# Token chunks of a channel attention with a gated feed-forward: twelve of 504 or 508 tokens instead of eleven of 512 and one of 448

## The chip, the cores and the metric

The kernel runs on one core of one Trainium2 chip. The metric is the device time of the execution in microseconds. A core has TensorE (PE: matmuls and their weight loads), VectorE (DVE), ScalarE (ACT), GpSimd (POOL) and SyncE (SP, which here issues the DMAs).

## The reference

Four batches of 6080 tokens and 256 channels. First an attention between channels, whose weights are a 256 x 256 matrix for each batch; then a feed-forward layer of width 2048 on every token.

```python
B, N, C = (4, 6080, 256)
qn = q / (np.linalg.norm(q, axis=1, keepdims=True) + 1e-06)
kn = k / (np.linalg.norm(k, axis=1, keepdims=True) + 1e-06)
s = kn.transpose(0, 2, 1) @ qn / tau
a = softmax(s)                      # [B, 256, 256]
x = (v @ a).reshape(B * N, C)
h = x @ w_in                        # w_in [256, 2048]
g = h * (1.0 / (1.0 + np.exp(-1.702 * h)))
return g @ w_out                    # w_out [2048, 256]
```

## The kernel before

**Layout.** Tokens run along the free dimension, channels and hidden units along the 128 partitions. `v` comes in transposed and the output leaves transposed. The attention matrix of a batch is folded into `w_in` (`weights`, line 413), so that the main loop computes hidden units straight from `v`. Every factor of a product is split into a high and a low part (`split`, lines 78 and 79: a cast on ScalarE and a subtraction on VectorE), and each product is three matmuls: high by high, high by low, low by high.

**Chunks.** The tokens of a batch are cut into chunks (line 62), 512 wide by `NCH`, with a last one of 448. `chunks[c]` is a pair of offset and width. All tiles for a chunk in SBUF and PSUM have room for 512 columns and are used up to the width `w`. `v_load` fetches a chunk of `v`, `v_split` splits it.

**The main loop.** `order` lists the slots of a batch: chunk by chunk, and for each the 16 blocks `f` of 128 hidden units. In the first batch the first two chunks go in turn, block by block. In each slot `hidden` issues six matmuls (line 456: two halves of the channels by three products), a sigmoid on ScalarE (line 462), a product on VectorE (line 463) and the split of the result into `gh` and `gl`. Two or three slots later `project` issues the six matmuls of line 484 (two halves of the output channels by three products), which add up over the 16 blocks in PSUM. After the last block the two halves are copied out (VectorE line 492, ScalarE line 494) and stored (line 496). A chunk is thus 16 slots of 12 matmuls.

**Side work.** `put` hangs other work on slots by their number: the load and split of the next chunk, the attention of the next batch (`prepare`, `score` with 512 and 256 columns at lines 285 and 294, norms, softmax, folded weights), and in the first batch the conversion of the 64-bit weights (lines 118 to 132). These numbers depend on `NCHUNK` and `NF` only.

**Order.** PE runs in the order that the code is written in (`manual_schedule` for PE). The other engines' order in the main loop is decided by the scheduler from its own estimate of the time line.

Of the kernel before, what the change touches and what calls it, by code (L numbers as in the profile page):

```python
# [22 lines left out]
NCH = 512  # L23
# [4 lines left out]
def channel_attention_then_glu(  # L28
# [21 lines left out]
    B, N, C = q.shape  # L50
# [8 lines left out]
    TAIL = N - T * P  # L59
    UT = 2  # L60
    RT = 4
    chunks = [(o, min(NCH, N - o)) for o in range(0, N, NCH)]
    NCHUNK = len(chunks)

    const = ctx.enter_context(tc.tile_pool(name="const", bufs=1))
    wp = ctx.enter_context(tc.tile_pool(name="wp", bufs=NG + 2))
# [546 lines left out]
    with tc.manual_schedule(engines={mybir.EngineType.PE}):  # L613
        for b in range(B):
            side = start if b == 0 else {}
            order = [(c, f) for c in range(NCHUNK) for f in range(NF)]
            if b == 0:
                order[: 2 * NF] = [(c, f) for f in range(NF) for c in range(2)]

            def put(s, fn, *a):  # L620
                side.setdefault(s, []).append((fn, a))

            for c in range(2 if b == 0 else 1, NCHUNK + (b + 1 < B)):
                at_v = (c - 1) * NF
                bc = (b, c) if c < NCHUNK else (b + 1, 0)
                if b == 0 and c == 2:
# [7 lines left out]
            if b + 1 < B:  # L634
# [26 lines left out]
                put(e + 16, nxt.transposes)  # L661
                total = NCHUNK * NF
                at_g = [total - 32, total - 24, total - NF + 5, total - NF + 10]
# [45 lines left out]
```

## Time and profile before

| | us |
|---|---|
| median of 3 runs | 2286.29 |
| lowest and highest | 2285.43, 2288.52 |
| the profiled execution | 2288.67 |
| its span, first to last instruction | 2286.9 |

A profile is one execution. Its page gives the busy time of each engine and the chain of work that ended last, followed back from the end. The views used below are the page, the groups of instructions by line with shapes kept apart (busy us, mean ns of one, idle time before), the waits of PE (us in total, times, longest), the busy time by stage (sum for PE, weight loads, VectorE, ScalarE, GpSimd, then PE's granted clock, the DMA share and GB/s), and the chain in order of time (start, length, what). Matmuls are pipelined: a matmul's own duration (391 ns at 512 columns) is longer than the distance from its start to the next one's start, so the pace is read from starts.

### The profile page before, as it was taken

The numbers are of one execution on the slowest core, as the hardware profiler recorded it, in microseconds if no ns is written. First come the engines' busy times: TensorE is split into PE (matmuls) and PEld (weight loads), VectorE is DVE, ScalarE is ACT, GpSimd is POOL, SyncE is SP. The second block draws the span as 40 slices with busy tenths as digits, with TensorE's granted clock in tenths as the row PEclk, the third lists the DMA queues.
The fourth block names the chain that finished last, engine by engine and source line by source line (L and its number), as shares of the span: only waits on it lengthen the run. The fifth ranks groups of instructions, "written<-read, shape, count | busy, mean of one in ns | idle before, by whom it ended". The sixth has DMA issues, their size and how long they took to land.

```text
span 2286.9 us, 27146 instructions
## 1 busy us (share of the span) xinstructions
PE 2277.1 (100%) x10256; PEld 1901.9 (83%) x10256; DVE 1379.7 (60%) x2073; ACT 1240.4 (54%) x2145; POOL 219.2 (10%) x160
## 2 busy tenths in 40 slices
PE   9999999999999999999999999999999999999999
PEld 7788888888888888888888888888888888888888
DVE  6976656755556665665555666666555555555554
ACT  6766555554555555555454555654554444444444
POOL 0012222200011222110000222300000000000000
PEclk9999999999999999999999999999999999999999
DMA  9311211100111112110011112110001000000000
GB/s 340 109 51 60 74 56 54 46 27 19 36 38 56 56 56 72 55 39 18 19 38 36 56 56 74 53 35 22 18 19 36 19 19 28 28 19 28 27 10 18
DMA packets 45812, 109.76 MB, mean 48 GB/s; under 512 B 4464, under 2 KB 7792, under 8 KB 45680
## 3 DMA queue, kind: packets, MB, share of 16 engines
q1 hardware_dynamic: 45680, 108.02, 14.1%
q8 instruction: 80, 1.31, 0.3%
q14 instruction: 52, 0.43, 0.1%
HBM read 83.10 MB, written 24.90 MB: 47 GB/s over the span
## 4 chain that ended last, share of the span: by engine, by line
PE 98%; DVE 1%; DMA 1%; ACT 0%; SPq 0%; issue 0%; ACTq 0%
PE ps_o L484 45%; PE ps_h L456 45%; PE s L285 3%; PE ps_w L413 2%; PE s L275 2%; PE s L294 1%; DMA raw_k<-in_k 0%; PE s_first L250 0%; DMA raw_q<-in_q 0%; DVE v_l L79 0%; SPq L206 0%; PE ps_n L312 0%; DVE gl L79 0%; DVE g L463 0%; ACT sq L238 0%
## 5 line engine op out<-in xcount | busy, mean ns | idle before, releaser
L79 DVE TENSOR_TENSOR gl<-g,gh 128x512 fp32r<-128x512 f32 (+1 forms) x768 | 548.2, 715 | 463.7 <-ACT gh L78 462.2
L78 ACT CAST gh<-g 128x512 fp32r<-128x512 f32 (+1 forms) x768 | 472.3, 615 | 503.5 <-DVE g L463 501.5
L463 DVE TENSOR_TENSOR g<-ps_h,g 128x512 f32<-128x512 f32 (+1 forms) x768 | 524.3, 684 | 345.6 <-ACT g L462 338.8
L462 ACT ACTIVATE g<-ps_h 128x512 f32<-128x512 f32 (+1 forms) x768 | 455.6, 593 | 419.7 <-PE ps_h L456 418.0
L456 PE MATMUL ps_h<-v_h,wh 128*128 128x512 f32 (+1 forms) x1536 | 596.9, 389 | 0.0
L484 PE MATMUL ps_o<-gl,wo_h 128*128 128x512 f32 (+1 forms) x1536 | 595.0, 387 | 1.4 <-DVE gl L79 1.4
L456 PE MATMUL ps_h<-v_l,wh 128*128 128x512 f32 (+1 forms) x1536 | 595.5, 388 | 0.0
L484 PE MATMUL ps_o<-gh,wo_h 128*128 128x512 f32 (+1 forms) x1536 | 594.8, 387 | 0.0
L456 PE MATMUL ps_h<-v_h,wl 128*128 128x512 f32 (+1 forms) x1536 | 594.9, 387 | 0.0
L484 PE MATMUL ps_o<-gh,wo_l 128*128 128x512 f32 (+1 forms) x1536 | 594.6, 387 | 0.0
L484 PEld LDWEIGHTS ps_o<-gl,wo_h 128*128 128x128 f32 x1536 | 288.3, 188 | 59.5 <-DVE gl L79 2.9
L456 PEld LDWEIGHTS ps_h<-v_h,wl 128*128 128x128 f32 x1536 | 288.3, 188 | 58.1 <-DVE wl L79 0.6
L484 PEld LDWEIGHTS ps_o<-gh,wo_h 128*128 128x128 f32 x1536 | 288.3, 188 | 57.9 <-ACT gh L78 0.5
L484 PEld LDWEIGHTS ps_o<-gh,wo_l 128*128 128x128 f32 x1536 | 288.3, 188 | 56.8
L456 PEld LDWEIGHTS ps_h<-v_h,wh 128*128 128x128 f32 x1536 | 288.6, 188 | 55.3
L456 PEld LDWEIGHTS ps_h<-v_l,wh 128*128 128x128 f32 x1536 | 288.7, 188 | 54.5
L240 POOL TENSOR_TENSOR acc_q<-acc_q,sq 128x512 f32<-128x512 f32 (+1 forms) x72 | 93.7, 1302 | 1110.8 <-ACT sq L238 1110.8
L240 POOL TENSOR_TENSOR acc_k<-acc_k,sq 128x512 f32<-128x512 f32 (+1 forms) x72 | 116.1, 1613 | 3.3 <-ACT sq L238 3.2
L79 DVE TENSOR_TENSOR v_l<-v_raw,v_h 128x512 fp32r<-128x512 f32 (+2 forms) x94 | 76.0, 847 | 4.6 <-ACT v_h L78 4.6
L285 PE MATMUL s<-qs,ks 128*128 128x512 f32 (+1 forms) x272 | 73.5, 390 | 0.0
L238 ACT ACTIVATE sq<-raw_q 128x512 f32<-128x512 f32 (+1 forms) x96 | 58.4, 609 | 21.4 <-DMA raw_q<-in_q 16.8
L238 ACT ACTIVATE sq<-raw_k 128x512 f32<-128x512 f32 (+1 forms) x96 | 58.1, 605 | 7.5 <-DMA raw_k<-in_k 3.3
(87 smaller groups left out, 896.3 us busy)
## 6 DMA issues: line engine op xcount, KB each, us to landing
v_raw<-in_vT SPq DMA_DIRECT2D x44, 512.0 KB, 3.8
out_T<-osb SPq DMA_DIRECT2D x88, 256.0 KB, 2.1
raw_q<-in_q SPq DMA_DIRECT2D x43, 512.0 KB, 3.8
raw_k<-in_k SPq DMA_DIRECT2D x43, 512.0 KB, 4.5
words<-in_w_in SPq DMA_DIRECT2D x8, 512.0 KB, 7.7
words<-in_w_out SPq DMA_DIRECT2D x8, 512.0 KB, 3.4
v_raw<-in_vT SPq DMA_DIRECT2D x4, 448.0 KB, 3.6
out_T<-osb SPq DMA_DIRECT2D x8, 224.0 KB, 2.0
```

What stands on the lines that cost most here:

```text
L78: ins = nc.scalar.copy(dst_hi, src)
L79: nc.vector.tensor_tensor(dst_lo, src, dst_hi.bitcast(F32), op=ALU.subtract)
L238: nc.scalar.activation(sq, r, AF.Square)
L240: eng.tensor_tensor(acc, acc, sq, op=ALU.add)
L275: nc.tensor.matmul(self.s[i][:, :C], lhsT=ks[:, j, i * P : (i + 1) * P], rhs=qs[:, j, :], start=u == start and j == 0, stop=last and j == ...
L285: nc.tensor.matmul(self.s[i], lhsT=ks[:pp, j, 0, i * P : (i + 1) * P], rhs=qs[:pp, j, :, :], start=u == start and j == 0, stop=False, skip ...
L294: nc.tensor.matmul(self.s[i][:, C:], lhsT=ks[:pp, j, 1, i * P : (i + 1) * P], rhs=qs[:pp, j, 0, :], start=False, stop=last and j == nt - 1 ...
L413: nc.tensor.matmul(ps, lhsT=l[:, j, ci], rhs=r[:, j, :], start=n == 0, stop=n == 3 * NC2 - 1,)
L456: nc.tensor.matmul(ps[:, :w], lhsT=l[:, j, fs], rhs=r[:, j, :w], start=n == 0, stop=n == 3 * NC2 - 1,)
L462: newest[0] = nc.scalar.activation(g, ps[:, :w], AF.Sigmoid, scale=1.702)
L463: nc.vector.tensor_tensor(g, ps[:, :w], g, op=ALU.mult)
L484: nc.tensor.matmul(out[d][:, :w], lhsT=l[:, f, ds], rhs=r[:, :w], start=f == 0 and n == 0, stop=f == NF - 1 and n == 2,)
```

## The change

The number of chunks is rounded up from the token count by 512, as before twelve. The cuts then lie at twelfths of the tokens, rounded down to a multiple of four: widths 504, 508, 508, four times over. Nothing else is edited; every place that uses a chunk reads offset and width from `chunks`.

```diff
-    chunks = [(o, min(NCH, N - o)) for o in range(0, N, NCH)]
-    NCHUNK = len(chunks)
+
+    NCHUNK = -(-N // NCH)
+    assert N % 4 == 0
+    cuts = [4 * (N // 4 * c // NCHUNK) for c in range(NCHUNK + 1)]
+    chunks = [(o, z - o) for o, z in zip(cuts, cuts[1:])]
+    assert max(w for _, w in chunks) <= NCH
```

Line numbers behind the edit are four higher. PE's order, in the last batch, where the last chunk's first slots stand between projections of the chunk ahead of it. Before:

```order
L456 MATMUL ps_h<-v_h,wh 128x448
L456 MATMUL ps_h<-v_l,wh 128x448
L456 MATMUL ps_h<-v_h,wl 128x448
L484 MATMUL ps_o<-gh,wo_h 128x512
L484 MATMUL ps_o<-gl,wo_h 128x512
L484 MATMUL ps_o<-gh,wo_l 128x512
```

PE's order at the same place now:

```order
L460 MATMUL ps_h<-v_h,wh 128x508
L460 MATMUL ps_h<-v_l,wh 128x508
L460 MATMUL ps_h<-v_h,wl 128x508
L488 MATMUL ps_o<-gh,wo_h 128x508
L488 MATMUL ps_o<-gl,wo_h 128x508
L488 MATMUL ps_o<-gh,wo_l 128x508
```

Nothing moves on PE; only widths differ, here and everywhere. The orders of SyncE and GpSimd are the same too.

VectorE's order in the first batch, while weights are converted (`z`, `words`, `eighths` and `win` belong to the conversion, `wl` and `wo_l` are split weights, `g` and `gl` the main loop's tiles). Before:

```order
L463 TENSOR_TENSOR g_675<-ps_h_668,g_675 128x512
L121 TENSOR_SCALAR z_691<-z_691 128x512
L79 TENSOR_TENSOR wo_l_101<-z_637,wo_h_100 128x512
L463 TENSOR_TENSOR g_708<-ps_h_701,g_708 128x512
L123 TENSOR_SCALAR z_691<-z_691 128x512
L79 TENSOR_TENSOR gl_679<-g_675,gh_678 128x512
L127 SCALAR_TENSOR_TENSOR z_691<-words_610,z_691 128x512
L79 TENSOR_TENSOR gl_712<-g_708,gh_711 128x512
```

VectorE's order at the same place now:

```order
L467 TENSOR_TENSOR g_675<-ps_h_668,g_675 128x504
L83 TENSOR_TENSOR gl_652<-g_648,gh_651 128x508
L125 TENSOR_SCALAR z_691<-z_691 128x512
L83 TENSOR_TENSOR wo_l_101<-z_637,wo_h_100 128x512
L83 TENSOR_TENSOR gl_679<-g_675,gh_678 128x504
L127 TENSOR_SCALAR z_691<-z_691 128x512
L467 TENSOR_TENSOR g_708<-ps_h_701,g_708 128x508
L131 SCALAR_TENSOR_TENSOR z_691<-words_610,z_691 128x512
```

The product for `g_708` has moved behind the split `gl_679` and a step of the conversion. There are about a dozen such exchanges on VectorE and about as many on ScalarE, nearly all in the first batch's first slots.

## The prediction

> **What bounds the kernel now.** I begin with the profile's page: how full each engine is, what clock TensorE was granted, and who holds the chain that ended last.
>
> ```profile
> span 2286.9 us, 27146 instructions
> PE 2277.1 (100%) x10256; PEld 1901.9 (83%) x10256; DVE 1379.7 (60%) x2073; ACT 1240.4 (54%) x2145; POOL 219.2 (10%) x160
> ...
> PEclk9999999999999999999999999999999999999999
> ...
> PE 98%; DVE 1%; DMA 1%; ACT 0%; SPq 0%; issue 0%; ACTq 0%
> ```
>
> TensorE is busy through the whole span, at the full clock, and 98% of the last chain is its own matmuls, one behind the other. Busy time alone proves little here, because ends of matmuls are modelled. So the second view is the waits of PE, and the third the busy time by stage.
>
> ```profile
> PE s L275 <- DMA raw_k<-in_k: 3.5, 3, 2.4
> PE ps_o L484 <- DVE gl L79: 1.4, 3, 0.9
> ...
> 65.00:140.00 75.00, 74.02 (x323) 60.20 (x322) 68.69 (x119) 51.84 (x91) 0.00 (x0) 1.00 0.27 85
> ...
> 1800.00:2200.00 400.00, 400.00 (x1766) 331.24 (x1765) 219.96 (x323) 193.82 (x324) 0.00 (x0) 1.00 0.08 24
> ```
>
> The largest waits of PE are 3.5 us and 1.4 us in the whole execution. In the last batch (the 400 us row: PE, weight loads, VectorE, ScalarE, GpSimd) VectorE is busy for 55% and ScalarE for 48%, so neither can hold PE. Only in the first batch, from 65 to 140 us, is VectorE nearly full (68.69 of 75 us), and even there PE lost 0.98 us. So the time is a count of matmuls times the **step** from one start to the next, and the question is what a step costs at 504 and 508 columns.
>
> The fourth view is the chain of waits near the end, in which each row is six matmuls (start, length, what). It covers the change from the last 512-column chunk to the 448-column chunk of the last batch.
>
> ```profile
> 2226.71 1.36 PE ps_h L456 x6
> ...
> 2238.95 1.36 PE ps_o L484 x6
> 2240.31 1.21 PE ps_h L456 x6
> 2241.53 1.38 PE ps_o L484 x6
> 2242.91 1.21 PE ps_h L456 x6
> ...
> 2249.31 1.22 PE ps_o L484 x6
> ...
> 2277.28 1.22 PE ps_h L456 x6
> ```
>
> From 2226.71 to 2238.95 lie nine groups of six at 512 columns: 12.24 us over 54 matmuls, **226.67 ns a step**. From 2249.31 to 2277.28 lie 23 groups of six at 448 columns: 27.97 us over 138 matmuls, **202.68 ns a step**. The step falls by 24.0 ns for 64 columns, 0.375 ns a column.
>
> A third width stands in the attention for the next batch: four matmuls of 256 columns (line 294) between ones of 512.
>
> ```profile
> 177.86 0.47 PE s L294 x4
> 178.34 1.39 PE ps_h L456 x6
> 179.72 1.36 PE ps_o L484 x6
> ```
>
> Four in 0.47 us are 117.5 ns each. From 256 to 512 columns the step thus grows by 109.2 ns, 0.426 ns a column. That straight line gives 199.4 ns at 448; the measured 202.68 is **3.3 ns above it**. So cutting columns off 512 did not return all that the line promises. The 1.39 us row shows the same from another side: six 512-column matmuls straight behind other widths took 231.7 ns each instead of 226.67, and the next six were back at 1.36. In the 448 transition the 512s between 448s took 1.38 (230 ns). A 512-column stream by itself holds the pace at which the line ends; whatever breaks it costs some ns.
>
> **The change part by part.** Widths first. 6080 tokens become eight chunks of 508 and four of 504 in each batch, in the place of eleven of 512 and one of 448. Chunks, slots, matmuls and weight loads keep their numbers, and the columns streamed are the same in sum. PE's order is the same, row by row.
>
> ```profile
> L456 PE MATMUL ps_h<-v_h,wh 128*128 128x512 f32 x1408 | 550.3, 391 | 0.0
> ...
> L456 PE MATMUL ps_h<-v_h,wh 128*128 128x448 f32 x128 | 46.7, 365 | 0.0
> ```
>
> There are six such groups of each width (three products at line 456, three at line 484): 8448 matmuls of 512 and 768 of 448 now; 6144 of 508 and 3072 of 504 after (8 or 4 chunks, 4 batches, 16 slots, 12 matmuls). Before: 8448 x 226.67 = 1914.9 us and 768 x 202.68 = 155.7 us, **2070.6 us** of the 2286.9.
>
> No row has a width of 504 or 508, so their step has to be bounded. From below by the line through 256 and 512: 226.67 - 4 x 0.426 = 224.96 and 226.67 - 8 x 0.426 = 223.26 ns, together 6144 x 224.96 + 3072 x 223.26 = 2068.0 us, **2.6 us less**. (By the flatter line through 448 and 512 the sum is the same as now to the last digit, since both the number of matmuls and the sum of columns stay.) From above by the row of disturbed 512s: 5.0 ns over the line, 9216 x 5.0 = 46.1 us on 2068.0, 43.5 us more than now. Between them lie two values. If 504 and 508 carry the 3.3 ns of 448, the sum is 2068.0 + 30.4, **27.8 us more**. If each takes just the step of a 512, because the few columns saved come back as a pause, the sum is 9216 x 226.67, which is the 768 narrow ones made 24.0 ns dearer: **18.4 us more**.
>
> I take the last one, the value of the nearest row: 504 and 508 are 4 and 8 columns from 512, where the line saves only 1.7 and 3.4 ns, and the one width that the trace has below 512 in a stream of its own gave 3.3 ns of its saving away. A saving no larger than that loss is likeliest to be eaten entire.
>
> Now the parts that I cost at nothing. VectorE and ScalarE get the same number of instructions:
>
> ```profile
> L79 DVE TENSOR_TENSOR gl<-g,gh 128x512 fp32r<-128x512 f32 x704 | 507.3, 721 | 425.2 <-ACT gh L78 423.7
> ...
> L79 DVE TENSOR_TENSOR gl<-g,gh 128x448 fp32r<-128x448 f32 x64 | 41.0, 641 | 38.5 <-ACT gh L78 38.5
> ```
>
> 80 ns for 64 columns, 1.25 ns a column, so 5 to 10 ns less an instruction on 508 or 504 and more on what was 448. Both engines idle nearly half the time, so PE hides it. In the first batch VectorE's order changes at some places between 65 and 140 us: a sigmoid product or a split passes a weight conversion or is passed by one. At most the 0.98 us that PE lost there could come back; if each of some seven exchanged pairs held PE for one instruction of 0.69 us, 4.8 us would be lost. The projection runs two or three tiles behind, 5 to 8 us, which covers one late instruction; I take zero. If that cover were gone, this is the price.
>
> Transfers: the rows shrink by 16 or 32 bytes.
>
> ```profile
> out_T<-osb SPq DMA_DIRECT2D x88, 256.0 KB, 2.1
> v_raw<-in_vT SPq DMA_DIRECT2D x4, 448.0 KB, 3.6
> ...
> out_T<-osb SPq DMA_DIRECT2D x8, 224.0 KB, 2.0
> ```
>
> A load of v (3.6 us here) is issued about a chunk ahead, 16 slots of 2.72 us or 43.5 us, and SP's order is unchanged, so even a doubled transfer is hidden. Only at the end is something bare: the last chunk is 508 wide instead of 448, so its copy takes about 60 ns more and its store 0.1 us more. That is +0.2 us, within the rounding. The matmuls of the attention and of the folded weights (512 and 256 columns) stay; their neighbours are narrower now, and a disturbed six costs 0.03 us as in the 1.39 row; some 70 places, so 2 us either way, in the range.
>
> **Sum.** The profiled execution took 2288.67 us, 1.77 us more than its span; with 18.4 us it becomes 2307.1. It was 2.4 us above the median of the three runs (2286.29). On the median I forecast **2304.7 us**, 0.8% slower.
>
> **The rivals.**
> *The line holds* (not slower). 504 and 508 keep pace at their own width: the same count times a straight price. For it: 256 columns do return most of their price. Against it: the 448 row. It gives 2283.7 to 2286.3. It decides if the step at these widths averages under 225.2 ns; above that the 0.2% (4.6 us, 0.5 ns a matmul) is passed.
> The Trainium skill, "TensorE: Matmul & The Clock Gate", section "Back-to-back issue gap", has such a line for single matmuls at the full clock: N divided by 2.4, plus 2.5 ns. By it 512 columns would be 215.8 ns and 448 columns 189.2, and the change would come to nothing; the trace has 226.67 and 202.68, a smaller step for the 64 columns, so it does not agree here.
>
> *The 448 surplus* (slower by more). A width that does not hold the pace of 512 pays 3.3 ns each: +27.8 us, 2314.1. For it: 448 paid this steadily over 138 matmuls. Against it: 448 is much farther from 512.
>
> *No beat at all* (slowest). Widths alternate between 504 and 508 in the first batch, and every step costs what a disturbed 512 costs: +43.5 us, 2329.8. For it: the 1.39 and 1.38 rows. Against it: those rows are back to 1.36 after one group.
>
> *VectorE's new order* holds PE in the first batch: up to +4.8 us on top of any of these, or -1.
>
> **How the numbers follow.** A 512 step: 0.42. The 448 surplus: 0.20. The line: 0.20. No beat: 0.12. The rest, 0.06, is a mix of line and surplus, or a gain that I don't see. A measurement can tell about 0.2% from no change. The range takes in the line's lower end, less the 0.98 us of the start, and the 448 surplus with 2 us for the disturbed places: 2283 to 2316; it leaves out the slowest case and a few hundredths. Slower by over 0.2% are the first, second and fourth case and half of the rest: 0.77. Within 0.2% is the line with part of the rest: 0.19. Faster by over 0.2%: 0.04.
>
> **What would show it.** In the changed kernel's chain of waits in the last batch, groups of six: 1.36 us at both widths says a 512 step; 1.34 (504) and 1.35 (508) the line; 1.36 and 1.37 the surplus; 1.37 and 1.38 no beat. Over a whole chunk of 192 matmuls the starts tell them apart. PE must still be busy throughout and its waits for VectorE must stay near 1.4 us in total; if they grow, the order in the first batch is the cause. I would be wrong altogether if groups of six fell below 1.34 us, or if PE waited for stores or loads of v.

## The result and the profile after

The changed kernel takes 2312.43 us (median of 4 runs, 2312.33 to 2314.45) against 2287.09 us before (4 runs). The ratio is **1.0113, 95% interval 1.0100 to 1.0125**: 25.3 us slower. The forecast was 2304.7 us with a range of 2283 to 2316.

The page of the changed kernel, its first lines and the chain by engine:

```profile
span 2310.6 us, 27145 instructions
PE 2301.7 (100%) x10256; PEld 1902.3 (82%) x10256; DVE 1381.6 (60%) x2073; ACT 1242.6 (54%) x2145; POOL 218.3 (9%) x160
...
PEclk9999999999999999999999999999999999999999
...
PE 98%; DMA 1%; DVE 1%; ACT 0%; SPq 0%; issue 0%; ACTq 0%
```

The same number of matmuls, the same clock, again 98% of the chain on PE. The span grew by 23.7 us, PE's busy time by 24.6, the other engines' by about 2 or not at all. Now the waits of PE (us in total, times, longest) and the busy time by stage:

```profile
PE s L279 <- DMA raw_k<-in_k: 2.8, 2, 2.5
...
PE ps_o L488 <- DVE gl L83: 0.9, 1, 0.9
```

```profile
65.00:140.00 75.00, 74.03 (x323) 60.05 (x322) 67.69 (x117) 51.75 (x90) 0.00 (x0) 1.00 0.26 81
1800.00:2200.00 400.00, 400.00 (x1760) 330.30 (x1760) 216.33 (x321) 190.88 (x320) 0.00 (x0) 1.00 0.08 24
```

PE waits less than before (0.9 us for VectorE against 1.4), and its share from 65 to 140 us is the same to a hundredth, so VectorE's new order cost nothing. In the last batch PE fits 1760 matmuls into 400 us, where it was 1766. The chain of waits shows at which width (groups of six: start, length, what). First a chunk of 504, then the last two chunks, of 508:

```profile
1792.51 1.36 PE ps_h L460 x6
1793.87 1.36 PE ps_o L488 x6
...
1797.95 1.36 PE ps_h L460 x6
```

```profile
2230.46 1.37 PE ps_o L488 x6
2231.83 1.37 PE ps_h L460 x6
...
2300.12 1.36 PE ps_h L460 x6
```

At 504 the groups stand at 1.36 us, as 512 did: 226.67 ns a matmul. At 508, 51 groups take 69.66 us: 69660 / 306 = **227.6 ns, more than at 512** (over a chunk the starts in nanoseconds give 227.61). Eight columns fewer cost the same, four columns fewer cost more. In nanoseconds the starts at 504 are 226 or 227 apart, but for a few at the edges of a chunk; at 508 they repeat 225, 230, 232, 233, 224, 227, 223, seven steps to a round, a nanosecond more or less.

The account: 3072 x 226.67 + 6144 x 227.61 = 2094.8 us, against 2070.6 before, 24.2 us of the 25.3. Another part is in a row whose own width did not change, the attention's 512-column matmuls, which stand behind 504s or 508s now. Before, this row was 71.3 us and 389 ns:

```profile
L289 PE MATMUL s<-qs,ks 128*128 128x512 f32 x266 | 72.5, 393 | 0.0
```

The two spans differ by less, 23.7 us, because TensorE ran at half clock for 3.4 us near the start of the profiled execution of before (mean clock 0.97 over the first 55 us, against 1.00 in that of after), about 1.7 us by estimate.

### The profile page after: what moved, and what is told of

Same layout as the page of the kernel before. It is cut to its first block, busy times and chain, and to the rows that moved or that the text cites. A ratio compares the mean times of both kernels' runs of the same rounds, so it can differ in the third digit from the quotient of the medians.

```text
span 2310.6 us, 27145 instructions
## 1 busy us (share of the span) xinstructions
PE 2301.7 (100%) x10256; PEld 1902.3 (82%) x10256; DVE 1381.6 (60%) x2073; ACT 1242.6 (54%) x2145; POOL 218.3 (9%) x160
## 4 chain that ended last, share of the span: by engine, by line
PE 98%; DMA 1%; DVE 1%; ACT 0%; SPq 0%; issue 0%; ACTq 0%
PE ps_o L488 45%; PE ps_h L460 45%; PE s L289 3%; PE ps_w L417 2%; PE s L279 2%; PE s L298 1%; DMA raw_k<-in_k 0%; PE s_first L254 0%; DMA raw_q<-in_q 0%; SPq L210 0%; PE ps_n L316 0%; DVE v_l L83 0%; DVE g L467 0%; PE ps_t L389 0%; PE ps_b L339 0%
## 5 line engine op out<-in xcount | busy, mean ns | idle before, releaser
L83 DVE TENSOR_TENSOR gl<-g,gh 128x508 fp32r<-128x508 f32 (+1 forms) x768 | 549.1, 716 | 473.1 <-ACT gh L82 471.4
L82 ACT CAST gh<-g 128x508 fp32r<-128x508 f32 (+1 forms) x768 | 472.5, 615 | 506.2 <-DVE g L467 504.5
L467 DVE TENSOR_TENSOR g<-ps_h,g 128x508 f32<-128x508 f32 (+1 forms) x768 | 523.6, 683 | 355.5 <-ACT g L466 348.6
L466 ACT ACTIVATE g<-ps_h 128x508 f32<-128x508 f32 (+1 forms) x768 | 455.6, 593 | 440.1 <-PE ps_h L460 438.6
L460 PE MATMUL ps_h<-v_h,wh 128*128 128x508 f32 (+1 forms) x1536 | 600.0, 391 | 0.0
L488 PE MATMUL ps_o<-gl,wo_h 128*128 128x508 f32 (+1 forms) x1536 | 598.1, 389 | 1.0 <-DVE gl L83 0.9
L488 PE MATMUL ps_o<-gh,wo_h 128*128 128x508 f32 (+1 forms) x1536 | 598.5, 390 | 0.0
L460 PE MATMUL ps_h<-v_h,wl 128*128 128x508 f32 (+1 forms) x1536 | 598.4, 390 | 0.0
L460 PE MATMUL ps_h<-v_l,wh 128*128 128x508 f32 (+1 forms) x1536 | 598.1, 389 | 0.0
L488 PE MATMUL ps_o<-gh,wo_l 128*128 128x508 f32 (+1 forms) x1536 | 597.9, 389 | 0.0
L242 ACT ACTIVATE sq<-raw_q 128x512 f32<-128x512 f32 (+1 forms) x96 | 58.4, 608 | 22.9 <-DMA raw_q<-in_q 18.4
```

The lines of the kernel that those rows point to most:

```text
L82: ins = nc.scalar.copy(dst_hi, src)
L83: nc.vector.tensor_tensor(dst_lo, src, dst_hi.bitcast(F32), op=ALU.subtract)
L242: nc.scalar.activation(sq, r, AF.Square)
L460: nc.tensor.matmul(ps[:, :w], lhsT=l[:, j, fs], rhs=r[:, j, :w], start=n == 0, stop=n == 3 * NC2 - 1,)
L466: newest[0] = nc.scalar.activation(g, ps[:, :w], AF.Sigmoid, scale=1.702)
L467: nc.vector.tensor_tensor(g, ps[:, :w], g, op=ALU.mult)
```

## The experiments

The question was why a narrower matmul takes no less time, and whether the width is the cause at all. I call A: the moving operand is paid in blocks of 32 columns counted from its address; B: in blocks from its own first column; C: a line with a surplus off 512; D: the width alone sets the step, irregularly; R: the step depends on how the address of the moving operand stands to that of the weights. Steps below are means over some 137 matmuls, start to start, in one chunk of the last batch, where no side work stands between.

**Thirteen widths in one kernel.**

```diff
-    chunks = [(o, min(NCH, N - o)) for o in range(0, N, NCH)]
+    widths = [512, 500, 496, 492, 488, 484, 480, 476, 464, 460, 456, 452, 320]
...
+    chunks = [(sum(widths[:c]), w) for c, w in enumerate(widths)]
```

> Thirteen chunks of 512, 500, 496, 492, 488, 484, 480, 476, 464, 460, 456, 452 and 320 columns in each batch, on the layout of before. Theory A (blocks by address): the moving operand is paid for in blocks of 32 columns, 13.33 ns each, counted from the tile's address; every moving tile of this program starts 24 columns past a block's edge, so a step is 13.33 ns times (width + 24) / 32 rounded up: 226.7 ns at 512, 500, 496 and 492; 213.3 ns at 488, 484, 480, 476, 464 and 460; 200.0 ns at 456 and 452; 146.7 ns at 320, with a surplus of a few ns at some of them as at 448 (202.7) and 508 (227.6). Theory B (blocks from the matmul's own first column): 226.7 ns from 512 down to 484, and 213.3 ns from 480 down to 452. Theory C (a line with a surplus of 3.3 ns off the pace of 512): a smooth fall of about 0.4 ns a column, 219.7 ns at 488 and 206.1 ns at 456. The total has 8% more matmuls and tells nothing by itself; A gives 205 blocks a slot row against 202.2 now, about 2316 us.

It took 2326.35 us (one run). The steps, with 448, 504 and 508 from the two kernels, and what is left over 0.4167 ns a column (the slope from 320 to 512, both constant steps):

| width | step ns | left ns | | width | step ns | left ns |
|---|---|---|---|---|---|---|
| 512 | 226.67 | 13.3 | | 476 | 213.34 | 15.0 |
| 508 | 227.61 | 15.9 | | 464 | 210.04 | 16.7 |
| 504 | 226.66 | 16.7 | | 460 | 206.66 | 15.0 |
| 500 | 223.32 | 15.0 | | 456 | 208.88 | 18.9 |
| 496 | 220.00 | 13.3 | | 452 | 206.64 | 18.3 |
| 492 | 219.99 | 15.0 | | 448 | 202.66 | 16.0 |
| 488 | 225.65 | 22.3 | | 320 | 146.67 | 13.3 |
| 484 | 218.66 | 17.0 | | | | |
| 480 | 216.70 | 16.7 | | | | |

The chain of this run, at 496 and then at 488:

```profile
1892.70 1.32 PE ps_h L458 x6
1894.02 1.32 PE ps_o L486 x6
```

```profile
1972.11 1.36 PE ps_h L458 x6
...
1974.80 1.36 PE ps_h L458 x6
```

At 488 a group takes what it takes at 504 or 512; at 496 it takes 0.04 us less. A wanted 213.3 ns at 488 and 226.7 at 496; both are off by 7 to 12 ns, so A falls, and B with it (226.7 at 496, 492 and 484). C's smooth fall is not there either. What stands out is a floor: 13.3 ns over the straight price, reached by 512, 496 and 320, and undercut by no lasting pace. (The 117.5 ns that the prediction read at 256 columns is not a lasting pace: the starts of those four are 114, 119, 120 and 120 ns apart, and 120.0 is 13.3 over the straight price too.)

The table holds for one chunk of each width, in the last batch. In the first three batches of the same run, between side work, some widths also held another pace for many matmuls on end: 488 at 220.0 ns, 492 at 222.2, 496 at 223.5, 500 at 226.7, 464 at 213.3, 460 at 208.9. At 512, 484, 480, 476, 456 and 452 the table's step came back in every batch. So a row of the table, that of 488 above all, need not be the only price of its width.

**No 508.** Eight chunks of 504 and four of 512 (`widths = [504, 504, 512] * 4`).

> Eight chunks of 504 and four of 512, so that 508 is absent. Theories A and B: each step is that of a 512, 226.67 ns, 18.4 us over before: 2305.5 us, 7 us under the changed kernel although the columns are the same in sum. Theory C (every width off 512 carries a surplus over the line): 504 at 226.6 ns and 512 at 226.7, the same 18 us, so C is told from A by the other runs; what this run tells is whether 508 alone makes up the rest of the 25.3 us. Rival: the pace suffers from alternating widths as such, then this stays near 2312 us.

2308.21 us, ratio 1.0092 (1.0075 to 1.0109), and 226.66 to 226.67 ns at both widths. So 504 costs a 512 step, and 508 adds most of the rest: the spans are 2305.2 here and 2310.6 with 508, 5.4 us apart. (The ratios, whose intervals overlap, are 4.8 us apart.)

**The same full width for all twelve.** The output is still cut at the changed kernel's places, but each chunk is computed as 512 columns.

```diff
+    kept = chunks
+    chunks = [(min(o, N - NCH), NCH) for o, _ in kept]
...
-                dst = outT[d * P : (d + 1) * P, b * N + o : b * N + o + w]
-                nc.sync.dma_start(dst, osb)
+                k, n = kept[c]
+                dst = outT[d * P : (d + 1) * P, b * N + k : b * N + k + n]
+                nc.sync.dma_start(dst, osb[:, k - o : k - o + n])
```

> The changed kernel's twelve output chunks of 504 and 508, but each computed as a full window of 512 tokens that overlaps its neighbour; only the 504 or 508 own columns are stored. 64 columns a batch are computed twice, on every engine. Theory D: every step is 226.67 ns, 18.4 us over before: about 2305 us, some 6 us FASTER than the changed kernel with 1% more columns. Rival E (the cost comes from cutting at odd offsets, from the transfers or from the new order on VectorE, which all stay): 2312 us or more.

**2305.94 us**, ratio 1.0083 (1.0068 to 1.0099), 0.4 us from the working out of a 512 step for every matmul (2287.1 + 18.4 = 2305.5). More columns on every engine, and 6.5 us faster than the changed kernel. The cuts, the stores of 504 and 508 columns and the number of columns on the other engines are not the cause. This run does not clear VectorE's new order. The expectation says that it stays, but in the trace it went back nearly to that of before: 8 of 2073 instructions stand elsewhere, against 36 that stand elsewhere than in the changed kernel. The run with tiles filled from the right, further down, does keep it.

**Every tile on a multiple of 128 bytes.** In the compiled programs all large tiles start 96 bytes past one. Padding three small constants moves all that stands behind them together.

```diff
-    half = const.tile([P, 2 * NC2], F32, name="half")
+    half = const.tile([P, 64], F32, name="half")[:, : 2 * NC2]
...
-    tau_sb = const.tile([P, 1], F32, name="tau_sb")
-    rtau = const.tile([P, 1], F32, name="rtau")
+    tau_sb = const.tile([P, 64], F32, name="tau_sb")[:, :1]
+    rtau = const.tile([P, 64], F32, name="rtau")[:, :1]
```

> The kernel before with three small constant tiles padded to 256 bytes, so that every tile behind them starts on a multiple of 128 bytes (32 columns) instead of 96 bytes past one. Nothing else moves. Theory A: a 512 touches 16 blocks instead of 17, a 448 touches 14 instead of 15.2: 213.3 and 186.7 ns, 8448 x 213.3 + 768 x 186.7 = 1945 us against 2070.6, 125 us less: about 2162 us if nothing else becomes late. Theories B and C, in which the address plays no part: 2287 us, no change.

> The changed kernel with the same padding. Theory A: 504 and 508 touch 16 blocks as 512 does: 9216 x 213.3 = 1966 us, about 2183 us, 20.5 us slower than the padded kernel before and 130 us faster than without the padding. Theories B and C: 2312 us, no change.

2287.04 us, ratio 1.0002 (0.9993 to 1.0012), and 2311.61 us, 1.0106 (1.0090 to 1.0121): nothing moved, and A, which promised 125 us, is done with. An address common to both operands plays no part.

**A better mix of widths.** `widths = [512] * 8 + [496] * 4`, both at the floor in the table.

> Eight chunks of 512 and four of 496, the two widths near 512 at which the run with thirteen widths showed a constant step of the width plus 13.3 ns (226.67 and 220.00 ns; 448 has 202.67, 508 has 227.6). Theory D (the step depends on the width alone, and only some widths hold the low price): 6144 x 226.67 + 3072 x 220.00 = 2068.5 us against 2070.6, 2.1 us less than before and 27 us less than the changed kernel, though twelve unequal chunks as well: 2284.6 us. Rival E (unequal or narrower chunks as such cost time): over 2290 us.

2288.85 us, ratio 1.0009 (1.0001 to 1.0018): no gain, a touch slower. The chain shows why. The second batch and the last, both at 496:

```profile
1030.01 1.34 PE ps_o L486 x6
1031.35 1.34 PE ps_h L458 x6
```

```profile
2171.11 1.32 PE ps_o L486 x6
2172.43 1.32 PE ps_h L458 x6
```

In the last batch 496 runs at 220.0 ns throughout. In the second it begins at 220.0 too. Behind four matmuls of 128 columns (line 337, at 1028 us) it goes over to 223.3 ns and keeps that for 73 us, the starts in one chunk 221, 223, 227 and 222 apart, over and over. The first six matmuls of line 415, at 1101 us, set it back to 220.0. In the first and the third batch the pace changes at the same two places. One width has two lasting paces, and what ran before it picks one. D is not enough: the width does not fix the step. The slower pace costs about 3.3 ns on some 330 matmuls in each of three batches, 3.3 us, more than the 2.1 us that were to be had.

**Weights of 64 columns** in line 484.

```diff
-            ds = slice(d * P, (d + 1) * P)
+            ds = slice(d * P, d * P + P // 2)
...
-                    out[d][:, :w], lhsT=l[:, f, ds], rhs=r[:, :w],
+                    out[d][: P // 2, :w], lhsT=l[:, f, ds], rhs=r[:, :w],
...
```

The copies and stores of the output are halved with it.

> The kernel before with weights of 64 columns instead of 128 in line 484; the lower half of each output half is left out. Theory F (the 13.3 ns over the straight price are the weight load of the next matmul, taken out of the same stream in proportion to its columns): 220.0 ns a step in line 484, 226.67 in line 456, 4608 x 6.67 = 31 us less, 2256 us. Theory G (a fixed price of a matmul, whatever its weights): 226.67 ns in both, 2287 us.

2300.29 us (one run): slower. A weight load fell from 188 to 134 ns, and yet the groups of line 484 grew:

```profile
L484 PEld LDWEIGHTS ps_o<-gl,wo_h 128*64 128x64 f32 x1536 | 206.6, 134 | 139.6 <-DVE gl L79 2.4
```

```profile
2002.06 1.36 PE ps_h L456 x6
2003.42 1.38 PE ps_o L484 x6
```

From start to start the steps of line 484 are 230.1 ns and those of line 456 226.5, between 1800 and 2200 us. F falls: the 13.3 ns are not in proportion to the weights' columns. G is not right either, since the step rose. Changing the weight load upset the pace of matmuls of an unchanged width, which pointed at something between the weight loads and the moving stream.

**Moving tiles shifted against the weights.** The first such run shifted the tiles within padded ones:

> The kernel before, with the moving tiles of chunk 0 to 10 (all 512 wide) started 0, 2, 4, 8, 12, 16, 20, 24, 28, 30 and 0 columns behind their old place, while the weights stay; one scratch buffer of the norms is taken away for room. Theory R (moving and weight reads collide by their relative address): the step of 512 columns differs from chunk to chunk, and at 24 columns, 96 bytes, the relation that line 413 has, it is near that line's 233.6 ns. Theory D (width alone): 226.67 ns in all eleven, 2287 us, and line 413 has another cause.

2326.15 us (one run), 231.0 to 234.0 ns in the shifted chunks, but 228.5 in the unshifted ones too: the padding had put the buffers 2176 bytes apart in place of 2048, so that a chunk mixed relations. It could not tell R from its own side effect, and I repeated it with buffers a multiple of 512 bytes apart.

```diff
+    shifts = [0, 8, 16, 24, 32, 48, 64, 96, 112, 4, 0, 0]
...
-            vh = vp.tile([P, NC2, NCH], F32R, tag="v_h", name="v_h")
+            vh = vp.tile([P, NC2 * NCH + 128], F32R, tag="v_h", name="v_h")[:, z : z + NC2 * NCH]
...
-        gh = (cv if there else gp).tile([P, NCH], F32R, tag="z" if there else "gh", name="gh")
+        gh = (cv if there else gp).tile([P, NCH + 128], F32R, tag="z" if there else "gh", name="gh")[:, z : z + NCH]
...
```

`v_l` and `gl` are shifted like `v_h` and `gh`.

> The kernel before, all of chunks 0 to 10 at 512 columns, with the moving tiles of chunk c started 0, 8, 16, 24, 32, 48, 64, 96, 112, 4 and 0 columns behind the old place. Unlike in the first run with shifts every buffer is a multiple of 512 bytes apart, and the scratch tiles of the weight conversion aren't used for the main loop, so that within a chunk moving tile and weights have one relation modulo 512 bytes, 0 in the kernel before. (The projection runs two slots behind throughout, and two rings are shorter, for room.) Theory R (the relation of the two read addresses sets the surplus): chunks 0 and 10 at 226.67 ns exactly, the shifted ones above it by up to 8 ns, each in a pattern of its own. Theory D (width alone; the first run's rise came from its other edits): 226.67 ns in all eleven.

All at 512 columns:

| shift, columns | 0 | 4 | 8 | 16 | 24 | 32 | 48 | 64 | 96 | 112 |
|---|---|---|---|---|---|---|---|---|---|---|
| step, ns | 226.66 | 231.68 | 233.31 | 228.86 | 233.35 | 233.37 | 233.35 | 226.66 | 233.37 | 233.35 |

The chain at a shift of 8, and at 64:

```profile
1858.21 1.40 PE ps_o L489 x6
1859.61 1.40 PE ps_h L460 x6
```

```profile
2079.81 1.36 PE ps_h L460 x6
2081.17 1.36 PE ps_o L489 x6
```

Same width, same order, same engines: 3% on every matmul from the place of one operand against the other. Shifts of 0 and 64 columns, 256 bytes apart, are alike, and so are the patterns of 32 and 96 (starts 229 and 237 or 238 ns apart in turn) and of 48 and 112 (230 or 231 and 235 or 236). R holds, D falls. The padded kernels above, where both operands moved by the same 160 bytes (modulo 256) and nothing changed, show that it is the place of one against the other that counts. (The run's total, 2337.29 us, has this in it.) At 24 columns the step is 233.35 ns, and line 413 had 233.6 in the kernel before. The two are not quite one relation: in the compiled program the weights of line 413 stand 96 bytes further on than its moving tiles, and a shift of 24 columns puts the moving tile 96 bytes further on than the weights. The Trainium skill, "TensorE: Matmul & The Clock Gate", section "Step-by-step: what each phase is for", says that loading the next weights takes no read bandwidth from the running matmul, since PE has two read ports. For these matmuls the runs don't agree, if it means that the two reads leave each other alone: where the operands stand to each other moves the step by up to 6.7 ns. What the two share, bandwidth or something else, is not shown.

**The same at 504 and 508.**

> The same on the changed widths 504, 508, 508: shifts of 8, 4, 4 (each chunk then ends where a 512 would end), 0, 8, 16, 4, 32, 64, 64, 0, 0 columns. Theory R with the end as what counts: 508 shifted by 4 and 504 shifted by 8 hold 226.67 ns or less. Theory R with the start as what counts: the unshifted ones stay at 226.67 (504) and 227.6 (508) and every shift costs more. Theory D: 226.67 and 227.6 whatever the shift.

508 shifted by 4 columns, so that it ends where a 512 ends: 226.7 ns in both chunks, against 227.6 unshifted. Shifted by 8, 16, 32 and 64: 230.47, 229.56, 228.88 and 227.61. 504 stayed at 226.7 with 0, 4, 8 or 64, where 512 lost 5.0 ns at a shift of 4 and 6.6 at 8; so the relation acts together with the width. A start off the old place is not what costs by itself; at 508 the common end with 512 brings back the 512 step.

**Two tests on whole kernels.** First the changed kernel, its tiles filled from the right, so that each stream ends with the tile:

```diff
-        split(vh[:, js, :w], vl[:, js, :w], raw[:, js, :w])
+        split(vh[:, js, NCH - w :], vl[:, js, NCH - w :], raw[:, js, :w])
...
-                    ps[:, :w], lhsT=l[:, j, fs], rhs=r[:, j, :w],
+                    ps[:, :w], lhsT=l[:, j, fs], rhs=r[:, j, NCH - w :],
...
-        split(gh[:, :w], gl[:, :w], g)
+        split(gh[:, NCH - w :], gl[:, NCH - w :], g)
...
-                    out[d][:, :w], lhsT=l[:, f, ds], rhs=r[:, :w],
+                    out[d][:, :w], lhsT=l[:, f, ds], rhs=r[:, NCH - w :],
```

> The changed kernel with its moving tiles filled from the right: the 504 or 508 columns lie at columns 8 to 511 or 4 to 511 of the 512-column tile, so that each stream starts 32 or 16 bytes later and ends where a 512 ends. Same widths, order, transfers and engine work. Theory R: as in the run with shifts, 226.63 ns at 508 and 226.67 at 504, 1.0 ns x 6144 = 6 us under the changed kernel: about 2306 us. Theory D (width alone): 2312 us.

**2305.27 us**, ratio to the kernel before 1.0081 (1.0066 to 1.0096), the steps as expected. 7 us of the 25 come back by where the columns lie, with no change of width. VectorE and ScalarE run in exactly the changed kernel's order here, so their new order has no part in these 7 us.

Second, the kernel before with line 413's weights moved into the main loop's relation:

```diff
-            m = small.tile([P, NC2], F32, tag="m", name="m")
+            m = small.tile([P, 48], F32, tag="m", name="m")[:, :NC2]
```

> The kernel before with one tile padded so that the transposed attention matrix, the weights of line 413, stands in the same relation modulo 256 bytes to its moving tiles as in the main loop, where it was 96 bytes off. Theory R: the 192 matmuls of line 413 fall from 233.6 ns to 226.7 or little more, 1.3 us less in all, too little for the clock of the runs but visible in the trace. Theory D: line 413 stays at 233.6 ns.

2286.26 us, ratio 0.9998 (0.9989 to 1.0007). Two rows of the chain before, and the two that answer in this run:

```profile
539.27 1.40 PE ps_w L413 x6
540.67 1.36 PE ps_h L456 x6
```

```profile
536.05 1.36 PE ps_w L413 x6
537.41 1.36 PE ps_h L456 x6
```

Line 413 is now at the main loop's pace in most of its groups: 122 of its 192 steps are 226 or 227 ns, where none was before. Over its 192 matmuls, those at the start among them, 44.85 us became 43.97, 0.9 us less where 1.3 were expected. This is too little for the clock; no kernel that I ran is measurably faster than the one before.

## Why the prediction came out as it did

**The bound was right.** PE holds the span before and after, no wait grew, and the result is a number of steps times their length.

**The zero terms were right.** VectorE's order, the loads and stores and the tail cost nothing that shows. One small thing was not: I wrote that VectorE's instructions would get 5 to 10 ns shorter; at 504 the split takes 705 ns in place of 721, but at 508 still 721:

```profile
L83 DVE TENSOR_TENSOR gl<-g,gh 128x508 fp32r<-128x508 f32 x512 | 368.7, 721 | 319.8 <-ACT gh L82 318.7
```

**The step of 508 was mis-sized.** The forecast gave 504 and 508 the step of 512. For 504 this is exact (226.67). 508 costs 227.61: 0.94 ns x 6144 = 5.8 us, most of the 6.9 us between the 18.4 forecast and the 25.3 measured. Another 1.2 us is in the attention's 512s (the 72.5 us row), which I had as "2 us either way".

**The reason behind the step was thin.** I argued that so small a saving would be eaten whole, from one row at 448. At 496 a saving of 16 columns is returned whole in the faster pace (220.00), and 508 is dearer than a 512, which eating the saving doesn't give. So the exact hit at 504 was luck as far as the reason goes. The 3.3 ns were misread as well: with the lasting 120.0 ns at 256 columns in place of 117.5, the line falls by 0.417 ns a column, 448 lies 2.7 ns above it, and the lower bound is 2.1 us less, not 2.6.

**The rival with the 448 surplus came nearer.** The prediction named groups of 1.36 and 1.37 us as its sign, and these are the groups that came. It put 508 at 224.96 + 3.3 = 228.3 ns, 0.7 above the measured step, where the forecast is 0.9 below; its total (+27.8 us) is 2.5 us off against 6.9. The range held the result because it took in this rival. But its form was wrong too: the surplus is no constant, it runs from nothing at 496 to 9 ns at 488 in the last batch, and it can be moved without touching the width.

**The other rivals.** The line did not hold at 504 or 508. At 496 it does (219.9 by its slope, 220.0 measured), at 320 nearly (144.9 and 146.7), so it was a fair rival. No beat at all did not come: the paces are locked patterns. The trace of the kernel before held the rows of line 413 (1.40 us a group, with no other width near), and I took disturbed neighbours for the only cause; those rows were the sign that the operands' places matter.

**What stays open.** The runs show that the step depends on the width, on the relation of the two operands modulo 256 bytes and on what ran just before. Why 504 columns take the step of 512 is not shown, and with the same step at 508 this makes 18.4 of the 25.3 us; no run here moved 504 off 226.7. A clash of the moving stream with the next weight load could fit all three, but it is a guess: no view shows it. Which widths hold the floor I cannot say by a rule; 512, 496 and 320 do, 480 and 448 were not seen to.

## What to carry to other kernels

Where TensorE holds the span, read the step from start to start for each width before cutting work into equal pieces: here eleven full widths and a rest cost less than twelve even ones, and computing 512 columns cost less than computing 508. Keep the moving tile and the weights in one relation (here equal modulo 256 bytes) and look for groups of one shape that run at two paces in one trace, since one padded tile can mend it, though here that returned only 0.9 us of TensorE's time, too little to show in the runs. When a width must be ragged, try which end of the tile it lies at: here that was worth 7 us.

## What I had not expected of the hardware

A shift of 8 columns of one operand against the other costs 6.6 ns on a step of 226.7, and 64 columns cost nothing. 488 columns took 225.65 ns in the last batch, where 496 took 220.00, and 220.0 in parts of the first. One width, 496, held 220.0 and 223.3 ns in one batch, and a few matmuls of other lines between were enough to change it. Halving the weights' columns made the step longer.
